# The keys' sums of four token tiles in one run, six weight sums moved from the keys into the perceptron, later numerators

## The chip, the cores and the metric

The kernel runs on one core of one Trainium2 chip. The metric is the time of one execution on the device in microseconds; lower is better. The engines are named as in the profile: PE (TensorE; PEld is its weight load), DVE (VectorE), ACT (ScalarE), POOL (GpSimd) and SP (SyncE, which here issues nearly all transfers; the ACT queue issues the stores of the queries' exponentials). Each of the first four works through its own queue in order, and so does SP.

## What is computed

A transformer block in fp32 on 2048 tokens of 1024 features: linear attention with a learned softmax feature map (32 heads of 32), then a perceptron of width 3584.

```python
def _A_ref(x, wqkv, w_phi, wo):
    q, k, v = qkv[0], qkv[1], qkv[2]
    pq = jnp.einsum("bhsd,hdf->bhsf", q, w_phi)
    pk = jnp.einsum("bhsd,hdf->bhsf", k, w_phi)
    phi_q = jnp.concatenate([_softmax(pq, axis=-1), _softmax(-pq, axis=-1)], axis=-1)
    phi_k = jnp.concatenate([_softmax(pk, axis=-1), _softmax(-pk, axis=-1)], axis=-1)
    kv = jnp.einsum("bhsf,bhsd->bhfd", phi_k, v)
    z  = jnp.einsum("bhsf->bhf", phi_k)
    num = jnp.einsum("bhqf,bhfd->bhqd", phi_q, kv)
    den = jnp.einsum("bhqf,bhf->bhq", phi_q, z)[..., None] + 1e-6
    o = num / den
    return (o as B, S, D) @ wo

h = x + _A_ref(_layernorm(x, axis=-1), A_wqkv, A_w_phi, A_wo)
h2 = h + relu(_layernorm(h) @ w1) @ w2
```

## The kernel before

**Products.** Every large product is made three times, from a high part and a remainder of each operand (mm3, L181 to L184: high by high, high by remainder, remainder by high), as matmuls of 128 x 128 by 128 x 512. Weights come raw from memory; ACT copies the high part (L125), and DVE or POOL makes the remainder (L129). Ten split weights (RW) and six raw ones (RR) are held. A matmul triple, one mm3, is a *step*; in the attention an item has eight steps, in the perceptron four. The work beside the products is put by hand at a step: `when(step, f, ...)` and `do(item, k, f, ...)` issue `f` there, and each engine then runs it in the order of issue, as soon as its inputs are there.

**Order of the stages.** Token tiles 0 to 7 (first half): keys and values in four slabs of 256 columns (items kv, 4 x 8), then queries in two slabs (items q, 2 x 8). Tiles 8 to 15 the same (second half, steps 384 to 767). Then the output product (wo, from step 768), which runs beside the attention's numerators, and from step 1024 (up0) the perceptron: first half `up_item`, 784 steps, second half `down_item`. The perceptron's products are of Strassen's kind with seven products (m in 1 to 7) of 2 x 2 blocks, so that some weight blocks are sums of blocks.

**Keys.** Per tile and slab: kv_first (L423; values to `vt`, maxima, minima and differences), kv_exp (11 steps after the item's start), kv_second (13; the map `kphi`), kv_z (18; POOL adds to the sums `zacc`) and kv_third (L456): eight small matmuls, run as 16 passes of 128x32 by 128x64, that add this tile's part of kv in two PSUM banks (`ac`). They need `vt` and `kphi` of that tile, and they stand at step 8(n + d) + 22 for item n, where d is 2, 1, 0, 2, 1, 0, 1, 0 over the eight tiles of a slab and half. So three, three and two tiles fall on one step. After the last slab z_sum (L484) and kv_turn (L478, L481) bring the sums into place.

**Weight sums.** t_load, t_sum and t_store (L348 to L366) make the sums of weight blocks that the perceptron's products use: per unit a load of 512 KB by SP, four subtractions on POOL (L363, 128 x 256 each, in place, in four consecutive steps), and a store of 512 KB by SP. There are 56 units, 28 of w1 and then 28 of w2; `sums_at` gives the step of each. The buffer is one of two pairs at a time (`b` in the pool tsum, `xn` of the layer norm, or `b` in the fold pool), by `home`.

**Attention.** at_load (L555; SP) brings a query unit u of 32 (512 KB); for some units the denominators are made early, in the keys' second half (EARLY: early_load, early_sums L582 on POOL, early_reduce L586 on DVE, at_cross, at_den, early_scale L590). at_scale (L629 and L634, POOL) divides, at_turn (L640, DVE) transposes, and at_num (L643, L653), for each odd u, makes the numerators of two units in two `ac` banks, which ACT (L660) and at_low (L670, DVE) bring into `oT`. For u < 8 the start of a unit is 8(last_kv + 4) + 19u // 2, and at_num stands 30 + `slack` steps after it. q_first (L514) needs one of two buffers `qe`, from which the ACT queue stores the exponentials (`ed`, L532); two tiles later the buffer is needed again.

**Perceptron, first half.** far_pair (L786) uses one buffer `y2` of the pool mp, for the second half of the tokens' layer norm; its last far_store stands at step up0 + 324.

Of the kernel before, what the change touches and what calls it, by code (L numbers as in the profile page):

```python
# [9 lines left out]
F32 = mybir.dt.float32  # L10
# [5 lines left out]
P = 128  # L16
S = 2048
D = 1024
# [4 lines left out]
HT = NT // 2  # L23
# [117 lines left out]
def kernel(  # L141
# [47 lines left out]
    def do(n, k, f, *args):  # L189
        at[n, k].append((f, args))  # L190
# [69 lines left out]
    fp_ln = kps.enter_context(tc.tile_pool(name="xn", bufs=2, side="right"))  # L260
    kp = kps.enter_context(tc.tile_pool(name="kp", bufs=2, side="right"))
    tsp = kps.enter_context(tc.tile_pool(name="tsum", bufs=1, side="right"))
    folds = ExitStack()
    fp = folds.enter_context(tc.tile_pool(name="fold", bufs=2))
# [82 lines left out]

    def t_load(w, p, j, home):  # L348
        cols = slice(256 * j, 256 * (j + 1))
        b = fp_ln.tile([P, D], F32, name="xn").rearrange("p (a f) -> p a f", a=4) if home == 2 else \  # L350
            (tsp, fp)[home].tile([P, 4, 256], F32, name="b", bufs=2)
        src = (w1 if w == 1 else w2)[2 * p:2 * p + 2, :, :, cols]
        sp.dma_start(b, src.rearrange("a b p f -> p (a b) f"))
        for r in range(2):
            for c in range(2):
                tsum[w, p, j, r, c] = b[:, 2 * c + r if w == 1 else 2 * r + c, :]
        tsum[w, p, j] = b
# [65 lines left out]
    def kv_first(key, ps):  # L423

        pk = ps[:, 0:256].rearrange("p (h f) -> p h f", f=32)
        vt = kp.tile([P, 256], F32, name="vt", bufs=5)
        act.activation(vt, ps[:, 256:512], AF.Copy)
        v_of[key] = vt
        m = kp.tile([P, 2, 8], F32, name="kmx", bufs=2)
        v.tensor_reduce(out=m[:, 0, :], in_=pk, op=ALU.max, axis=AX.X)  # L430
        v.tensor_reduce(out=m[:, 1, :], in_=pk, op=ALU.min, axis=AX.X)
        e = kp.tile([P, 8, 2, 32], F32, name="ke", bufs=2)
        v.tensor_sub(e[:, :, 0, :], pk, m[:, 0, :, None].to_broadcast([P, 8, 32]))
        v.tensor_sub(e[:, :, 1, :], m[:, 1, :, None].to_broadcast([P, 8, 32]), pk)
        e_of[key] = e
# [4 lines left out]
    def kv_second(key):  # L440
        e = e_of.pop(key).rearrange("p h s f -> p (h s) f")
        sm = kp.tile([P, 16], F32, name="ksm", bufs=2)
        v.tensor_reduce(out=sm, in_=e, op=ALU.add, axis=AX.X)
        v.reciprocal(sm, sm)
        phi = kp.tile([P, 16, 32], F32, name="kphi", bufs=4)
        v.tensor_mul(phi, e, sm[:, :, None].to_broadcast([P, 16, 32]))
        phi_of[key] = phi.rearrange("p h f -> p (h f)")

# [57 lines left out]
    def kv_item(key, keys):  # L506
        ps = yield from project(key[2], keys)
        kv_first(key, ps)
# [441 lines left out]
    def item(gen, *args, keys):  # L950
        items.append((gen, args + (keys,)))
        steps.extend((k,) for k in keys)
        return len(items) - 1
# [11 lines left out]
    for b, tiles in enumerate(groups):  # L965
        for hf in range(2):

            pairs = b == 0 and hf == 0
            for j in range(0, 4, 2 if pairs else 1):
# [3 lines left out]
                for half in range(2):  # L973
                    n = item(wo_pair, tiles[j:j + 2], hf, half, keys=[("wo", hf, 4 * half + k // 2) for k in range(8)])
# [26 lines left out]
    def when(step, f, *args):  # L1001

        if step < 8 * first_up:
            do(step // 8, step % 8, f, *args)
        else:
            do(first_up + (step - 8 * first_up) // 4, step % 4, f, *args)
# [4 lines left out]
    for t in range(1, NT):  # L1011
        n = t - 1 if t < HT else q_n[1, t - HT] + 1
# [34 lines left out]
    for (hf, s, t), n in kv_n.items():  # L1047
        when(8 * n + 11, kv_exp, (hf, s, t))
        when(8 * n + 13, kv_second, (hf, s, t))
        when(8 * n + 18, kv_z, (hf, s, t))  # L1050
        when(8 * (n + (2, 1, 0, 2, 1, 0, 1, 0)[t % HT]) + 22, kv_third, (hf, s, t))
        if hf == 1 and t == NT - 1:
            do(n + 3, 7, z_sum, s)
            do(n + 3, 7, kv_turn, s)
# [67 lines left out]
    for (sl, t), n in q_n.items():  # L1122
# [3 lines left out]
        b, i = place_of[t]  # L1126
# [2 lines left out]
            when(8 * n + (48, 48, 48, 72)[b], sm_load, b)  # L1129
    for u in range(32):  # L1130
        start = 8 * (a0 + u) - 4 if u >= 8 else 8 * (last_kv + 4) + 19 * u // 2
        slack = 6 if u < 6 else 4 if u >= 8 else 0
        late_ = 0 if u < 8 or u in EARLY else 3

        for step, f, *args in ((-8, at_load), (6, at_sums, 0), (10, at_reduce, 0), (9, at_sums, 1), (12, at_reduce, 1),
                               (14 + late_, at_cross), (16 + late_, at_den), (18 + late_, at_inverse), (20 + late_, at_scale),
                               (26 if u < 8 else 27, at_turn)):
            if u not in EARLY or f in (at_load, at_scale, at_turn):
                when(max(start + step, 8 * (last_kv + 4)), f, u, *args)
        if u % 2:  # L1140
            when(start + 30 + slack, at_num, u)
            when(start + 32 + slack, at_low, u)
        if u in EARLY:
            slab, after = EARLY[u]
            start = 8 * (kv_n[1, slab, NT - 1] + 4) + after
            for step, f in ((0, early_load), (9, early_sums), (14, early_reduce), (17, at_cross), (20, at_den), (22, early_scale)):
                when(start + step, f, u)
# [22 lines left out]
    up0 = 8 * first_up  # L1170
# [12 lines left out]
    def up_step(b, p, m):  # L1183

        return up0 + 4 * (up_n[b, p, m] + 1 - first_up)

    for j, m in enumerate(UP):

        for g in range(2):
            step = up0 + (8 * j + (-62, -29)[g] if j < 4 else 6 * (j - 4) + 4 + 2 * g)  # L1190
# [4 lines left out]
            step = up_step(0, NP - 1, m) + 2 * j  # L1195
# [4 lines left out]
    for b in range(2):  # L1200
# [7 lines left out]

    sixth, fifth = (10, 19, 28, 37, 46, 55), (10, 21, 32, 43, 54)
    sums_at = [30, 39, 47, 55] + [64 * i + k for i in (1, 2, 3) for k in sixth] + \  # L1210
        [266, 276, 286, 296, 332, 342, 352, 362, 372] + [64 * i + k for i in (6, 7, 8, 9) for k in (sixth, fifth)[i % 2]] + [638, 646, 655]
    for n, (w, p, j) in enumerate((w, p, j) for w in (1, 2) for p in range(NP) for j in range(2)):
        step = sums_at[n]
        half_on = sums_at.index(64 * 6 + 10)
        home = (0, 0, 1, 1)[n % 4] if step < 236 else (0, 0, 2, 2)[(n - half_on) % 4] if n >= half_on else 0
        when(step - (7 if 256 < step < 400 else 15), t_load, w, p, j, home)
        for k in range(4):
            when(step + k, t_sum, (w, p, j), k)
        when(step + 6, t_store, w, p, j)

    for b in range(2):
        for m in DOWN:
            n = down_n[b, m, NP - 1] + 1
            name, more = {1: "x1", 5: "x4", 6: "x2", 4: "x3"}.get(m), \
# [109 lines left out]
```

## Time and profile before

| | us |
|---|---|
| median of 3 runs | 1869.45 (1868.44 to 1871.39) |
| the profiled execution | 1867.49 |
| its span, first to last instruction | 1865.7 |
| PE busy | 1855.9 (99%) |
| DVE busy | 1065.1 (57%) |
| POOL busy | 978.9 (52%) |
| ACT busy | 770.9 (41%) |

Times inside the trace count from the first instruction. The stages in the trace: keys of the first half up to about 220 us, queries to about 330, keys of the second half to about 520, queries to about 608, output product to about 795, perceptron to 1329 and 1866. PE's busy time holds overlapping matmuls, so that 99% doesn't say that each runs at its best; the distance from one start to the next says more. The granted clock is 1.00 throughout. A row of the timeline gives start, duration, engine, line, operation, output and inputs, shape and count, and in brackets the idle time before and what ended it. A row of waits gives who waited for whom, the total in us, how often, and the longest.

### The profile page before, as it was taken

To read this page: it belongs to the slowest core of one execution; us is meant where nothing else is said; L and a number is where in the kernel's file an instruction comes from. 1 tells how busy PE (TensorE), PEld (TensorE's weight loads), DVE (VectorE), ACT (ScalarE), POOL (GpSimd) and SP (SyncE) were. 2 spreads that over 40 slices of the span, in tenths; PEclk is the share of its full clock that TensorE was granted. 3 is DMA by queue.
4 is the path that set the end of the run, shared out by engine and by line. 5 is a ranking of instruction groups with operands and counts; after the bars stand their busy time and mean duration, and the time that the engine had idled before them with its cause. 6 is when DMAs were issued, how large, how long until landed. Compare 5 with 4: busy or idle time off the path is not lost.

```text
span 1865.7 us, 28872 instructions
## 1 busy us (share of the span) xinstructions
PE 1855.9 (99%) x10088; PEld 1515.6 (81%) x10088; DVE 1065.1 (57%) x1651; ACT 770.9 (41%) x1379; POOL 978.9 (52%) x987
## 2 busy tenths in 40 slices
PE   9999999999999999999999999999999999999999
PEld 7777788887777777888888888888888888888887
DVE  7787678678679877575555653453434333343333
ACT  5322244233333343355455554444444444444442
POOL 4887745889956988343333222222344444444443
PEclk9999999999999999999999999999999999999999
DMA  7888799666676776888888976666677777777775
GB/s 229 288 292 285 237 288 266 194 196 201 209 229 194 247 244 206 283 271 231 248 257 265 328 240 184 194 206 198 229 222 215 216 218 238 237 218 215 216 217 177
DMA packets 334722, 435.13 MB, mean 233 GB/s; under 512 B 28784, under 2 KB 194672, under 8 KB 334576
## 3 DMA queue, kind: packets, MB, share of 16 engines
q1 hardware_dynamic: 300784, 416.51, 71.8%
q10 hardware_dynamic: 33792, 16.78, 3.1%
q8 instruction: 79, 1.29, 0.3%
q14 instruction: 67, 0.55, 0.1%
HBM read 295.31 MB, written 137.89 MB: 232 GB/s over the span
## 4 chain that ended last, share of the span: by engine, by line
PE 94%; DVE 3%; POOL 1%; issue 1%; ACT 0%; DMA 0%; SPq 0%; POOLq 0%; DVEq 0%
PE mm L182 24%; PE mm L183 24%; PE mm L184 24%; PE ac L182 4%; PE ac L184 4%; PE ac L183 4%; PE tp L182 2%; PE tp L183 2%; PE tp L184 2%; PE tp L246 1%; PE ac L465 1%; PE ac L653 1%; POOL w L129 1%; DVE qsm L537 1%; DVE qe L524 0%
## 5 line engine op out<-in xcount | busy, mean ns | idle before, releaser
L129 POOL TENSOR_TENSOR w<-raw,w 128x512 fp32r<-128x512 f32 x353 | 470.4, 1335 | 689.0 <-ACT w L125 664.3
L125 ACT ACTIVATE w<-raw 128x512 fp32r<-128x512 f32 x686 | 408.5, 626 | 506.9 <-PE mm L184 232.0
L129 DVE TENSOR_TENSOR w<-raw,w 128x512 fp32r<-128x512 f32 x333 | 269.1, 808 | 510.5 <-ACT w L125 504.6
L182 PE MATMUL mm<-w,xT 128*128 128x512 f32 x768 | 305.4, 398 | 0.0
L183 PE MATMUL mm<-w,xT 128*128 128x512 f32 x768 | 299.9, 391 | 1.0 <-POOL w L129 0.6
L184 PE MATMUL mm<-w,xT 128*128 128x512 f32 x768 | 299.3, 390 | 0.0
L183 PE MATMUL mm<-hT,w 128*128 128x512 f32 x672 | 261.4, 389 | 0.0
L182 PE MATMUL mm<-hT,w 128*128 128x512 f32 x672 | 261.4, 389 | 0.0
L184 PE MATMUL mm<-hT,w 128*128 128x512 f32 x672 | 261.4, 389 | 0.0
L182 PEld LDWEIGHTS mm<-w,xT 128*128 128x128 f32 x768 | 144.2, 188 | 34.9 <-issue 3.7
L184 PEld LDWEIGHTS mm<-w,xT 128*128 128x128 f32 x768 | 144.2, 188 | 30.7
L183 PEld LDWEIGHTS mm<-w,xT 128*128 128x128 f32 x768 | 144.3, 188 | 30.2 <-POOL w L129 1.2
L363 POOL TENSOR_TENSOR b<-b 128x256 f32<-128x256 f32 x176 | 143.5, 816 | 48.1 <-DMA b<-in_w_dram 39.9
L182 PE MATMUL mm<-w 128*128 128x512 f32 x392 | 152.5, 389 | 0.0
L183 PE MATMUL mm<-w 128*128 128x512 f32 x392 | 152.5, 389 | 0.0
L184 PE MATMUL mm<-w 128*128 128x512 f32 x392 | 152.5, 389 | 0.0
L183 PEld LDWEIGHTS mm<-hT,w 128*128 128x128 f32 x672 | 126.2, 188 | 26.2
L184 PEld LDWEIGHTS mm<-hT,w 128*128 128x128 f32 x672 | 126.2, 188 | 26.2
L182 PEld LDWEIGHTS mm<-hT,w 128*128 128x128 f32 x672 | 126.2, 188 | 26.1
L184 PEld LDWEIGHTS mm<-w 128*128 128x128 f32 x392 | 73.6, 188 | 15.3
L182 PEld LDWEIGHTS mm<-w 128*128 128x128 f32 x392 | 73.6, 188 | 15.3
L183 PEld LDWEIGHTS mm<-w 128*128 128x128 f32 x392 | 73.6, 188 | 15.2
(173 smaller groups left out, 3107.5 us busy)
## 6 DMA issues: line engine op xcount, KB each, us to landing
raw<-t SPq DMA_DIRECT2D x224, 256.0 KB, 3.9
raw<-ad SPq DMA_DIRECT2D x196, 256.0 KB, 3.0
raw<-in_w_dram SPq DMA_DIRECT2D x168, 256.0 KB, 3.1
ad<-c SPq DMA_DIRECT2D x112, 256.0 KB, 3.6
b<-in_w_dram SPq DMA_DIRECT2D x44, 512.0 KB, 5.7
t<-b SPq DMA_DIRECT2D x44, 512.0 KB, 5.0
ad<-s SPq DMA_DIRECT2D x84, 256.0 KB, 3.8
ed<-qe ACTq DMA_DIRECT2D x64, 256.0 KB, 4.6
```

The source lines that it names most:

```text
L125: nc.scalar.activation(w[:, 0, :], raw[1], AF.Copy)
L129: eng.tensor_tensor(out=w[:, 1, :], in0=raw[1], in1=w[:, 0, :].bitcast(F32), op=ALU.subtract)
L182: pe.matmul(ps, a_hi, b_hi, start=first, stop=False, skip_group_check=more)
L183: pe.matmul(ps, a_hi, b_lo, start=False, stop=False, skip_group_check=more)
L184: pe.matmul(ps, a_lo, b_hi, start=False, stop=last, skip_group_check=more)
L246: pe.transpose(pt[:, k, :], xn[:, (4 * j + k) * P:(4 * j + k + 1) * P], ident)
L363: pool.tensor_tensor(out=tsum[*u, *out], in0=tsum[*u, *a], in1=tsum[*u, *b], op=ALU.subtract)
L465: pe.matmul(kv_ps[s][g][32 * i:32 * (i + 1), 0:64], vt[:, 32 * h:32 * (h + 1)], phi[:, 64 * h:64 * (h + 1)], start=first, stop=last)
L537: v.tensor_reduce(out=sm[:, 0].rearrange("p s (a c) -> p a s c", a=4), in_=e_of.pop((s, t)), op=ALU.add, axis=AX.X)
L653: pe.matmul(banks[g][32 * c:32 * (c + 1), 256 * j:256 * (j + 1)], kvL[rows, 2 * q + h // 4, 32 * (h % 4):32 * (h % 4 + 1)], phT_of[u - 1 + ...
```

## The change

Four edits.

1. kv_third stands at 8(n + 3 - t % 4) + 22: tiles 0 to 3 of a slab and half fall on one step, and tiles 4 to 7. `vt` has six buffers instead of five, `kphi` five instead of four.
2. In the second half's keys the weight sums stand five to a slab in the second and third slab (six in the third before), three in the last (five before), and the three at the steps 638, 646 and 655 are no longer there.
3. Six units, the last of w2, stand in the perceptron's first half, at up0 + 480 + 36i, with the buffer y2.
4. The slack of u = 6 and 7 is 6 instead of 0. at_num is there for odd u alone, so at_num(7) and at_low(7) stand six steps later.

```diff
     def t_load(w, p, j, home):
         cols = slice(256 * j, 256 * (j + 1))
-        b = fp_ln.tile([P, D], F32, name="xn").rearrange("p (a f) -> p a f", a=4) if home == 2 else \
-            (tsp, fp)[home].tile([P, 4, 256], F32, name="b", bufs=2)
+        if home > 1:
+            b = fp_ln.tile([P, D], F32, name="xn") if home == 2 else mp.tile([P, D], F32, name="y2", bufs=1)
+            b = b.rearrange("p (a f) -> p a f", a=4)
+        else:
+            b = (tsp, fp)[home].tile([P, 4, 256], F32, name="b", bufs=2)
...
-        vt = kp.tile([P, 256], F32, name="vt", bufs=5)
+        vt = kp.tile([P, 256], F32, name="vt", bufs=6)
...
-        phi = kp.tile([P, 16, 32], F32, name="kphi", bufs=4)
+        phi = kp.tile([P, 16, 32], F32, name="kphi", bufs=5)
...
-        when(8 * (n + (2, 1, 0, 2, 1, 0, 1, 0)[t % HT]) + 22, kv_third, (hf, s, t))
+        when(8 * (n + (3 - t % 4)) + 22, kv_third, (hf, s, t))
...
         start = 8 * (a0 + u) - 4 if u >= 8 else 8 * (last_kv + 4) + 19 * u // 2
-        slack = 6 if u < 6 else 4 if u >= 8 else 0
+        slack = 6 if u < 8 else 4
...
     sixth, fifth = (10, 19, 28, 37, 46, 55), (10, 21, 32, 43, 54)
     sums_at = [30, 39, 47, 55] + [64 * i + k for i in (1, 2, 3) for k in sixth] + \
-        [266, 276, 286, 296, 332, 342, 352, 362, 372] + [64 * i + k for i in (6, 7, 8, 9) for k in (sixth, fifth)[i % 2]] + [638, 646, 655]
+        [266, 276, 286, 296, 332, 342, 352, 362, 372] + [64 * i + k for i, places in ((6, sixth), (7, fifth), (8, fifth), (9, (14, 28, 44))) for k in places] + \
+        [up0 + 480 + 36 * i for i in range(6)]
     for n, (w, p, j) in enumerate((w, p, j) for w in (1, 2) for p in range(NP) for j in range(2)):
         step = sums_at[n]
         half_on = sums_at.index(64 * 6 + 10)
-        home = (0, 0, 1, 1)[n % 4] if step < 236 else (0, 0, 2, 2)[(n - half_on) % 4] if n >= half_on else 0
+        home = 3 if step > up0 else (0, 0, 1, 1)[n % 4] if step < 236 else (0, 0, 2, 2)[(n - half_on) % 4] if n >= half_on else 0
         when(step - (7 if 256 < step < 400 else 15), t_load, w, p, j, home)
```

## The prediction

> **What bounds the kernel now.** I read the page first, then TensorE's own waits, then the busy time by stage, then the timelines where those waits fall.
>
> ```profile
> span 1865.7 us, 28872 instructions
> PE 1855.9 (99%) x10088; PEld 1515.6 (81%) x10088; DVE 1065.1 (57%) x1651; ACT 770.9 (41%) x1379; POOL 978.9 (52%) x987
> ...
> PE ac L653 <- DVE qe L640: 1.6, 1, 1.6
> ...
> PE ac L465 <- ACT w L125: 0.7, 1, 0.7
> PE mm L183 <- POOL w L129: 0.6, 1, 0.6
> ...
> PE tp L481 <- DVE kd L475: 0.3, 1, 0.3
> ```
>
> TensorE is busy for 99% of the span. Beside the first 17 us it waits at four places, all quoted. Only two things can shorten this kernel: those four waits, and work that fills TensorE's stream without being one of the large matmuls. The stream has a fixed beat, which a stage without small matmuls shows:
>
> ```profile
> 330.00:520.00 190.00, 189.02 (x1316) 150.99 (x1315) 133.32 (x258) 63.90 (x144) 169.75 (x169) 1.00 0.63 197
> ...
> 795.00:1329.00 534.00, 534.00 (x2386) 442.06 (x2385) 270.67 (x335) 264.63 (x447) 151.91 (x113) 1.00 0.77 234
> ```
>
> The columns after the length are busy time (and count) of PE, PEld, DVE, ACT and POOL. In the perceptron's first half (the lower row) 2386 matmuls less 32 tiny ones take 534.0 us: 0.227 us each, at clock 1.00; a step of three is 0.68 us. POOL is at 28% there, and at 89% in the second half of the keys (the upper row).
>
> **The keys' sums (kv_third).** Nothing is removed: 1024 passes stay 1024. Only the number of times changes that TensorE leaves the large matmuls for them.
>
> ```profile
> L465 PE MATMUL ac<-kphi,vt 128*32 128x64 f32 x1024 | 19.5, 221 | 0.7 <-ACT w L125 0.7
> ...
> 79.66 0.39 PE L184 MATMUL mm<-w,xT 128*128 128x512 f32 x1
> 79.98 0.65 PE L465 MATMUL ac<-kphi,vt 128*32 128x64 f32 x32
> 80.56 0.50 PE L182 MATMUL mm<-w,xT 128*128 128x512 f32 x1
> 80.90 0.40 PE L183 MATMUL mm<-w,xT 128*128 128x512 f32 x1
> ...
> 96.78 0.39 PE L184 MATMUL mm<-w,xT 128*128 128x512 f32 x1
> 97.10 0.88 PE L465 MATMUL ac<-kphi,vt 128*32 128x64 f32 x48
> ...
> 98.25 0.40 PE L183 MATMUL mm<-w,xT 128*128 128x512 f32 x1
> ...
> 99.20 0.39 PE L184 MATMUL mm<-w,xT 128*128 128x512 f32 x1
> ```
>
> A token tile is 16 passes (1024 over 64 tiles). Two tiles in a run: from the last large matmul before to the second after, 80.90 - 79.66 = 1.24 us, less two beats (0.45) = 0.79 us. Three tiles: 98.25 - 96.78 = 1.47, less 0.45 = 1.02 us. So a tile costs 0.23 us, and a run of any length 0.33 us more. The next four matmuls come at 0.2375 instead of 0.227 (98.25 to 99.20), another 0.04. Before, eight tiles of a slab and half go in runs of 3, 3 and 2; after, in 4 and 4, so each of the eight slab halves loses one run: 8 x 0.33 = 2.6 us at least, 8 x 0.37 = 3.0 at most. I take **2.9**, near the upper end, because the tail is seen behind the run.
>
> The first tile of a group now waits eight steps longer for its sum, which is why the buffers of vt and kphi grow by one each (1 KB and 2 KB of a partition). The last tile of each group keeps its distance: its kphi is made at step 13 after its item's start, its sum goes at 22. The fifth kphi buffer is written again at step 53 of a half, and the run that frees it stands at 46: seven steps or 4.8 us, as before (45 against 38). I cost that at nothing; if DVE were to wait there, only its kphi would come later, and TensorE reads that nine steps on.
>
> **The sums off the slab edge.** In the second half of the keys 25 weight sums (t_sum, four instructions each) become 19: one fewer in the third slab, two fewer in the last, and the three at its end are gone. Each is 4 x 0.74 us on POOL:
>
> ```profile
> 330.00:520.00 190.00, 73.66 (x89) 1.00 0.63 197
> ...
> 505.18 0.74 POOL L363 TENSOR_TENSOR xn<-xn 128x256 f32<-128x256 f32 x1
> 506.41 2.40 POOL L582 TENSOR_TENSOR xl<-xl,zb 128x1024 f32<-128x1024 f32 x1
> ...
> 508.85 1.22 DVE L586 TENSOR_REDUCE xtz<-xl 128x32 f32<-128x1024 f32 x1 [2.01 <-POOL xl L582]
> 510.99 0.71 DVE L446 TENSOR_TENSOR kphi<-ke,ksm 128x512 f32<-128x512 f32 x1
> ...
> 510.73 0.43 PE L465 MATMUL ac<-kphi,vt 128*32 128x64 f32 x16
> ...
> 512.20 0.50 PE L182 MATMUL mm<-w,xT 128*128 128x512 f32 x1
> ...
> 518.93 0.35 DVE L590 RECIPROCAL smx<-qden 128x32 f32<-128x32 f32 x1 [4.84 <-POOL qden L621]
> ```
>
> The first row is those sums alone: 73.7 us of POOL's 169.75. Six fewer take about 17.7 us from it. At the end of the last slab POOL runs late, the early queries' product (L582) stands behind sums, DVE's reduction waits for that, and the last tile's kphi stands behind the reduction, until 511.70. TensorE, at 511, waits. That run of 32 takes 1.47 us from its start to the next large matmul (510.73 to 512.20), against 0.58 at the undisturbed one above (79.98 to 80.56), so the wait costs **0.9**; TensorE's own row counts 0.7 of it, the lower end. With the sums of steps 630 and 638 gone from POOL's queue ahead of L582, kphi should come 3 to 4 us sooner, and in a run of four the last tile is read another 0.5 us later. The wait of L481 for kd has the same origin: ahead of kd in DVE's queue stands a reciprocal that waits 4.84 us, to 518.93, for a quotient that POOL delivers behind the same sums. It goes too: **0.3**.
>
> **The second query slab.** SyncE and ScalarE queues are passed here as well:
>
> ```profile
> 523.30 0.51 SPq L366 DMA_DIRECT2D t<-b  x1
> 523.86 5.80 SPq L555 DMA_DIRECT2D qe<-ed  x5
> ...
> 538.11 0.69 DVE L523 TENSOR_TENSOR qe<-mm,qmx 128x512 f32<-128x512 f32 x1 [5.43 <-DMA ed<-qe]
> ...
> 545.33 3.24 ACT L125 ACTIVATE w<-raw 128x512 fp32r<-128x512 f32 x6 [1.00 <-PE mm L184]
> ...
> 550.49 0.39 PE L182 MATMUL mm<-w,xT 128*128 128x512 f32 x1
> 551.83 0.40 PE L184 MATMUL mm<-w,xT 128*128 128x512 f32 x1
> ```
>
> SyncE stores the last sum at 523.30, once POOL has made it, and only then issues five loads of the attention (at_load). They share the DMA engines with the stores of the queries' exponentials (ed); one of those lands late, and DVE idles 5.43 us for its buffer. ScalarE stands in order behind those exponentials, so the six weight copies of the second query slab begin at 545.33, and POOL's remainders after them come late: two beats take 1.34 us instead of 0.45, **0.9** lost. Without the three sums SyncE is free of that store; the loads go as soon as the keys' buffers under them are free, between the last kv_third (512.2) and the turn that follows at 519.8: 4 to 12 us earlier, while DVE still has slack to catch up. I take the whole 0.9; the other end is nothing.
>
> **The later numerators.** Only u = 7 is odd with slack 0, so at_num(7) and at_low(7) go from steps 760 and 762 to 766 and 768.
>
> ```profile
> 580.54 1.09 PE L653 MATMUL ac<-qe,kvL 64*32 64x256 f32 x32
> 581.56 0.50 PE L182 MATMUL mm<-w,xT 128*128 128x512 f32 x1
> ...
> 590.62 0.66 PE L653 MATMUL ac<-qe,kvL 64*32 64x256 f32 x16
> 593.44 0.50 PE L182 MATMUL mm<-w,xT 128*128 128x512 f32 x1
> ...
> 591.60 1.19 DVE L640 STREAM_TRANSPOSE qe<-qe 128x1024 f32<-128x1024 f32 x1
> ```
>
> The run that waits takes 2.82 us, an undisturbed one 1.02: **1.8** lost, since DVE ends the transpose at 592.79. Six steps are 4.1 us, more than the lateness of 2.2, so the wait goes even if nothing else improves. What is late next: at_low(7) now stands behind the last query's maxima on DVE (four of 0.68) and its product is read at step 780, 12 steps or 8.2 us after 768. It needs some 3.6 us. Covered, unless DVE is more than 4.5 us late.
>
> **The six sums in the perceptron's first half.** They add six loads and six stores of 512 KB to SyncE's queue, and 17.7 us to POOL, in bursts of 3 us every 36 steps (24.5 us). What hides them (a stretch of that stage, 1122 to 1250 us):
>
> ```profile
> ACT w L125 <- PE mm L184: 25.3, 17, 1.6
> ...
> L129 POOL TENSOR_TENSOR w<-raw,w 128x512 fp32r<-128x512 f32 x23 | 30.2, 1314 | 94.9 <-ACT w L125 90.9 <-DMA ad<-s 4.0
> ```
>
> ScalarE's copies wait for TensorE to free one of ten weight places, so a weight is split about nine units (4 steps each, 24 us) ahead of its use. A burst of 3 us, and a store that holds SyncE for it, stay inside that. I cost it at nothing; without the cover, 17.7 us. The tile y2, which the loads use, is stored for the last time at step 324 of the stage; the first load stands at 465. What POOL still has to spare there is in the last row: 94.9 of 128 us.
>
> **Sum.** 2.9 + 0.9 + 0.3 + 0.9 + 1.8 = 6.8 us. The profiled execution took 1867.5, which gives 1860.7; it was 2.0 below the median of the runs shown (1869.45), and the median gives **1862.6**.
>
> **The rivals.** *The collision moves instead of going.* The attention's loads, earlier, meet the ed store of an earlier query tile; DVE idles as before and the weights of the second query slab stay late: 1862.6 + 0.9 = 1863.5; if at_num(7) still waits as well, 1865.3. For it: the loads' 2.5 MB do not shrink. The Trainium skill, DMA: Bandwidth & Descriptors, Issuing engines are not separate DMA queues, says that transfers started by different engines interleave on the same 16 DMA engines; the 5.43 us above agree. Against it: DVE also idles 4.8 us ahead of that stretch in the trace of before, which it can now use.
>
> *VectorE is the bound from 541 to 611.*
>
> ```profile
> 541.00:611.00 70.00, 67.83 (x431) 52.33 (x430) 68.45 (x102) 29.03 (x53) 49.52 (x59) 1.00 0.70 206
> ```
>
> DVE is busy for 68.45 of these 70 us, so what TensorE gains ahead of it could come back as a wait further on, and only the changeovers stay: 1869.45 - 2.9 = 1866.6. Against: the 5.4 us of idling lie just before.
>
> *The changeovers are priced by the pass, not by the run.* Then only the waits go: 1869.45 - 3.9 = 1865.5. The two rows above speak against it.
>
> *Slower: POOL's sums block VectorE in the perceptron.* In the keys it looks so:
>
> ```profile
> 498.83 1.48 DVE L446 TENSOR_TENSOR kphi<-ke,ksm 128x512 f32<-128x512 f32 x1
> ```
>
> The same instruction took 0.71 us at 510.99, with POOL idle. If each of the 24 new instructions held up one of DVE's and TensorE felt all of it, 24 x 0.74 = 17.7 us, less the 6.8: 1880.3. It decides from 10.5 us on, 0.44 for each. Against: DVE idles half of that stage and TensorE never waits in it. The Trainium skill, SBUF — State Buffer, Who interferes with whom, makes this a rule: an instruction of VectorE with two SBUF inputs and one of GpSimd that reads SBUF shut each other out until the first ends. The two kphi rows agree; no row here shows TensorE waiting for it.
>
> **How the numbers follow.** Forecast 0.68, the collision moves 0.15, VectorE bound 0.07, no cheaper changeovers 0.06, slower 0.04. About 0.2% (3.7 us) is what a measurement of this kernel can tell from no change. The forecast and most of the first rival are faster by more; the third is at the line; the second is within: 0.84, 0.12, 0.04. The low end takes every term at its upper end (7.0) and 1.4 of spread between runs; the high end reaches the VectorE rival: 1861.0 to 1866.5.
>
> **What would show it.** Runs of kv_third of 64 passes, 16 of them, each some 1.25 us; no wait of TensorE left at L465, L481, L183 and L653 between 500 and 600 us; the at_load row before 520 us, no idling of several us on DVE for ed; six groups of L363 on y2 after 1100 us with TensorE gapless. Wrong, if a new wait stands in the perceptron, or if DVE's idling for ed only moves.

## The result, and the profile after

| | before | after |
|---|---|---|
| median of ten runs, us | 1869.52 (1868.32 to 1872.12) | 1864.66 (1864.36 to 1865.06) |
| ratio | | 0.9971 (95%: 0.9963 to 0.9980) |
| span of the profiled execution, us | 1865.7 | 1862.7 |

The change gains 4.9 us by the medians; 6.8 were forecast. The two profiled executions differ by 3.0 us only, because the one of before took 1867.49 us, less than any of its ten timed runs. What follows compares traces, so its terms add up to about 3.

The page of the changed kernel, and TensorE's waits in it:

```profile
span 1862.7 us, 28867 instructions
PE 1852.3 (99%) x10088; PEld 1515.2 (81%) x10088; DVE 1069.7 (57%) x1651; ACT 771.3 (41%) x1379; POOL 982.0 (53%) x987
...
PE tp L246 <- ACT xn L239: 2.4, 1, 2.4
PE tp L1257 <- POOL ones L1253: 1.6, 1, 1.6
PE mm L183 <- POOL w L129: 1.0, 3, 0.7
PE mm L183 <- DVE w L129: 0.8, 1, 0.8
PE ac L656 <- DVE qe L643: 0.4, 1, 0.4
PE mm L183 <- POOL w L404: 0.4, 1, 0.4
```

From L351 on, the lines stand three or four lower than before (kv_third is now L468, at_num L656). The waits at kv_third and at kd are gone, and that at the numerators fell from 1.6 to 0.4. But L183, a matmul that reads a weight's remainder, now waits four times for POOL or DVE instead of once (the row with L404 is the start of the kernel). So part of the gain became other waits. Where, the start of the same large matmul in each trace shows (us; the last column is the fastest kernel of the experiments):

| step | before | after | difference | e8 |
|---|---|---|---|---|
| 0 | 13.40 | 13.71 | +0.31 | 13.51 |
| 384, keys of the second half | 311.42 | 312.07 | +0.65 | 310.10 |
| 640, queries | 500.31 | 499.37 | -0.94 | 496.80 |
| 704, second query slab | 547.08 | 545.12 | -1.96 | 542.55 |
| 712 | 554.69 | 551.80 | -2.89 | 549.24 |
| 768, output product | 598.33 | 593.61 | -4.72 | 591.04 |
| 1024, perceptron | 794.72 | 791.69 | -3.04 | 787.28 |
| last | 1861.62 | 1858.57 | -3.05 | 1854.16 |

The difference at the first row is the landing of the first tokens, which is not the change's: DVE begins on their second half at 5.38 us before and at 5.68 after. Over the traces of this document the first large matmul stands anywhere from 13.3 to 14.2 us, and at 15.6 in e7, where the granted clock is also 0.50 from 9.73 to 13.13 us.

The keys: one of the new runs, and a slab's edge (timeline, TensorE, then POOL):

```profile
104.20 0.39 PE L184 MATMUL mm<-w,xT 128*128 128x512 f32 x1
104.52 1.10 PE L468 MATMUL ac<-kphi,vt 128*32 128x64 f32 x64
...
105.89 0.40 PE L183 MATMUL mm<-w,xT 128*128 128x512 f32 x1
...
169.79 0.39 PE L182 MATMUL mm<-w,xT 128*128 128x512 f32 x1
170.84 0.50 PE L183 MATMUL mm<-w,xT 128*128 128x512 f32 x1 [0.67 <-POOL w L129]
...
167.92 1.18 POOL L366 TENSOR_TENSOR b<-b 128x256 f32<-128x256 f32 x1
169.07 2.97 POOL L129 TENSOR_TENSOR w<-raw,w 128x512 fp32r<-128x512 f32 x2
```

A run of 64 passes takes 105.89 - 104.20 - 0.45 = 1.24 us (1.25 forecast). At 170 TensorE is at step 196, the fifth weight of a new slab, and waits: POOL was still at a weight sum until 169.10 and made two remainders after it. Such a wait, with a slower first beat behind it, stands at the steps 132, 196 and 452 (0.46, 0.95 and 0.46 us in all), and two smaller ones, 0.14 and 0.10 us, at 263 and 582; before there was none of them.

The queries (timeline of SP, DVE and ACT):

```profile
513.54 9.84 SPq L558 DMA_DIRECT2D qe<-ed  x5
...
522.02 0.69 DVE L526 TENSOR_TENSOR qe<-mm,qmx 128x512 f32<-128x512 f32 x1 [2.32 <-DMA ed<-qe]
...
540.55 4.09 ACT L125 ACTIVATE w<-raw 128x512 fp32r<-128x512 f32 x6 [2.54 <-PE mm L184]
```

The attention's loads start 10.3 us sooner (513.54 against 523.86). DVE's idling for ed is 2.3 instead of 5.4 us and comes 16 us earlier, while there is slack; the second query slab's weight copies now wait for TensorE, as they should, and TensorE has no wait at step 709. (The row of before, at 545.33, names TensorE as well, for 1.00 us. There ScalarE's queue issued two stores of ed from 544.36 to 545.29, and the six copies then ran without a gap: it was late, not waiting.)

The start of the output product (timeline of PE and DVE):

```profile
603.14 0.39 PE L182 MATMUL mm<-w,oT 128*128 128x512 f32 x1
604.36 0.50 PE L183 MATMUL mm<-w,oT 128*128 128x512 f32 x1 [0.83 <-DVE w L129]
604.70 0.40 PE L184 MATMUL mm<-w,oT 128*128 128x512 f32 x1
605.02 0.66 PE L656 MATMUL ac<-qe,kvL 64*32 64x256 f32 x16
606.10 0.67 PE L656 MATMUL ac<-qe,kvL 64*32 64x256 f32 x16 [0.41 <-DVE qe L643]
606.70 0.50 PE L182 MATMUL mm<-w,oT 128*128 128x512 f32 x1
...
602.17 1.20 DVE L540 TENSOR_REDUCE qsm<-qe 128x32 f32<-128x1024 f32 x1
603.40 0.35 DVE L541 RECIPROCAL qsm<-qsm 128x32 f32<-128x32 f32 x1
603.67 0.63 DVE L129 TENSOR_TENSOR w<-raw,w 128x512 fp32r<-128x512 f32 x1
```

at_num(7) no longer waits: 2.9 us less up to step 761, of which 1.1 is its run itself, which stands later. But 15 steps on TensorE waits for a weight whose remainder DVE makes at 603.67, behind the queries' reductions: from 603.14 to 604.70, less two beats, 1.1 us. at_num(9), right behind, takes 1.68 us (605.02 to 606.70) instead of 1.02. So 1.76 of the 1.8 us come back.

Busy time in the three stages shown of before (us, busy of PE, PEld, DVE, ACT, POOL), and the six moved units on POOL:

```profile
330.00:520.00 190.00, 189.81 (x1328) 153.15 (x1327) 136.87 (x267) 66.60 (x149) 155.88 (x152) 1.00 0.57 176
541.00:611.00 70.00, 68.76 (x435) 53.21 (x434) 67.50 (x95) 30.52 (x56) 49.66 (x59) 1.00 0.69 211
795.00:1329.00 534.00, 534.00 (x2386) 442.22 (x2385) 271.26 (x334) 264.95 (x448) 170.11 (x135) 1.00 0.80 245
...
L366 POOL TENSOR_TENSOR y<-y x24: 727/742/1185, 1118.5 to 1246.4; 128x256 f32<-128x256 f32 x24
```

In the perceptron POOL has 18.2 us more to do (170.11 against 151.91) and TensorE 2386 matmuls in 534.00 us, as before. From step 1024 to the last large matmul it takes 1066.9 us in both.

### The profile page after: what moved, and what is told of

Same layout as the page of the kernel before. It is cut to its first block, busy times and chain, and to the rows that moved or that the text cites. A ratio compares the mean times of both kernels' runs of the same rounds, so it can differ in the third digit from the quotient of the medians.

```text
span 1862.7 us, 28867 instructions
## 1 busy us (share of the span) xinstructions
PE 1852.3 (99%) x10088; PEld 1515.2 (81%) x10088; DVE 1069.7 (57%) x1651; ACT 771.3 (41%) x1379; POOL 982.0 (53%) x987
## 4 chain that ended last, share of the span: by engine, by line
PE 93%; DVE 4%; POOL 1%; issue 1%; ACT 0%; DMA 0%; SPq 0%; POOLq 0%; DVEq 0%; ACTq 0%
PE mm L182 24%; PE mm L183 24%; PE mm L184 24%; PE ac L182 4%; PE ac L184 4%; PE ac L183 4%; PE tp L184 2%; PE tp L183 2%; PE tp L182 2%; PE tp L246 1%; PE ac L468 1%; POOL w L129 1%; PE ac L656 1%; DVE qsm L540 1%; DVE qe L643 0%
## 5 line engine op out<-in xcount | busy, mean ns | idle before, releaser
L129 DVE TENSOR_TENSOR w<-raw,w 128x512 fp32r<-128x512 f32 x333 | 274.0, 823 | 511.0 <-ACT w L125 502.0
L183 PE MATMUL mm<-w,xT 128*128 128x512 f32 x768 | 300.2, 391 | 1.4 <-POOL w L129 1.0
L183 PE MATMUL mm<-hT,w 128*128 128x512 f32 x672 | 261.7, 389 | 0.0
L183 PEld LDWEIGHTS mm<-w,xT 128*128 128x128 f32 x768 | 144.4, 188 | 31.8 <-POOL w L129 2.8
L366 POOL TENSOR_TENSOR b<-b 128x256 f32<-128x256 f32 x164 | 134.3, 819 | 49.4 <-DMA b<-in_w_dram 32.3
L183 PE MATMUL mm<-w 128*128 128x512 f32 x392 | 152.6, 389 | 0.0
L183 PEld LDWEIGHTS mm<-hT,w 128*128 128x128 f32 x672 | 126.2, 188 | 26.2
L183 PEld LDWEIGHTS mm<-w 128*128 128x128 f32 x392 | 73.6, 188 | 15.2
```

The source lines that it names most:

```text
L129: eng.tensor_tensor(out=w[:, 1, :], in0=raw[1], in1=w[:, 0, :].bitcast(F32), op=ALU.subtract)
L183: pe.matmul(ps, a_hi, b_lo, start=False, stop=False, skip_group_check=more)
L366: pool.tensor_tensor(out=tsum[*u, *out], in0=tsum[*u, *a], in1=tsum[*u, *b], op=ALU.subtract)
```

## The experiments

The comparison is with the kernel before, run beside each; the interval is that of the ratio. Where a run is set against the changed kernel or against e8, the two ran at different times (e9 and e10 also on another chip than e1 to e8), and their intervals overlap or touch. There the traces decide, and "by the traces" means from the first large matmul to the last.

**e1: the runs of four alone**

```diff
-        vt = kp.tile([P, 256], F32, name="vt", bufs=5)
+        vt = kp.tile([P, 256], F32, name="vt", bufs=6)
-        phi = kp.tile([P, 16, 32], F32, name="kphi", bufs=4)
+        phi = kp.tile([P, 16, 32], F32, name="kphi", bufs=5)
-        when(8 * (n + (2, 1, 0, 2, 1, 0, 1, 0)[t % HT]) + 22, kv_third, (hf, s, t))
+        when(8 * (n + (3 - t % 4)) + 22, kv_third, (hf, s, t))
```

> The kernel before with the keys' sums in runs of four tiles (and the larger vt and kphi) alone. Theory: sixteen runs of 64 passes instead of 24 of 48 and 32 save 0.40 us in each of eight slab halves, 3.2 us; but the run that stood two steps ahead of a slab's edge (step 62) had given POOL and DVE time for the next slab's weights, so that without it TensorE waits at the fifth weight of a new slab, some 2 us in all as in the changed kernel (steps 132, 196, 256, 452): about 1.1 us faster than before. Rival: those waits come from the moved weight sums, not from the runs: 3.2 us faster, and no wait at steps 132 and 196.

1866.32 us against 1869.02, ratio 0.9989 (0.9981 to 0.9998). Among its waits:

```profile
PE mm L183 <- POOL w L129: 1.6, 5, 0.7
```

The ratio's interval holds both expectations (0.4 to 3.6 us); the median gains 2.7 us, nearer to the rival's 3.2, and by the traces it is 0.9. The trace decides on the cause: the waits at the steps 132, 196 and 452 are here, of the same size (jumps of 0.34, 0.83 and 0.35 us against before), without a moved weight sum. They come with the runs. Another 1.3 us is lost at the steps 645 to 647, at the edge to the queries' first slab, where the changed kernel, with fewer sums there, loses nothing.

One thing more, which neither expectation has: the wait at 551 us (step 709) is gone here too (0.89 us), although SyncE issues the attention's loads at 524.81, no earlier than before. DVE's idling for ed is 4.1 us in two pieces instead of 5.4 in one.

**e2: the moved weight sums alone**, shown against the changed kernel

```diff
-        vt = kp.tile([P, 256], F32, name="vt", bufs=6)
+        vt = kp.tile([P, 256], F32, name="vt", bufs=5)
-        phi = kp.tile([P, 16, 32], F32, name="kphi", bufs=5)
+        phi = kp.tile([P, 16, 32], F32, name="kphi", bufs=4)
-        when(8 * (n + (3 - t % 4)) + 22, kv_third, (hf, s, t))
+        when(8 * (n + (2, 1, 0, 2, 1, 0, 1, 0)[t % HT]) + 22, kv_third, (hf, s, t))
-        slack = 6 if u < 8 else 4
+        slack = 6 if u < 6 else 4 if u >= 8 else 0
```

> The kernel before with the moved weight sums alone (six in the perceptron's first half, fewer near the ends of slabs). Theory: the waits at 511, 519 and 551 us go (0.9, 0.3 and 0.9), the one at at_num(7) stays at 1.5 to 2 us because DVE is as late there, and no wait comes at a slab's edge in the keys: 1.8 to 2.2 us faster. Rival: the waits at the slabs' edges are the sums' doing: they appear here too, and the gain is near nothing. In the perceptron's first half TensorE has no wait by both.

1864.95 us, ratio 0.9978 (0.9969 to 0.9987): 4.1 us. In the trace the three waits go (jumps of -0.89, -0.46 and -0.90 us at the steps 655, 664 and 709), there is none at a slab's edge, a small one is new (0.4 us at step 939, in the output product), and the one at at_num(7) falls by 0.91 instead of staying:

```profile
PE ac L656 <- DVE qe L643: 0.7, 1, 0.7
```

That last gain was not expected in this size: DVE, ahead of the queries, makes up part of its lateness. The medians show more than the 2.8 us of the traces, as with the whole change.

**e3: the later numerators alone**

```diff
-        slack = 6 if u < 6 else 4 if u >= 8 else 0
+        slack = 6 if u < 8 else 4
```

> The kernel before with the later numerators of u = 7 alone. The prediction's step: 1.8 us faster, since nothing is late next. Theory: VectorE is 6 us late at the start of the output product, so the wait goes from at_num(7) to the weights of the output product and to at_num(9), 12 to 20 steps later, at about the same price: within 0.5 us of before.

1869.26 us against 1869.02, ratio 0.9998 (0.9989 to 1.0007): nothing. The prediction's step falls. The timeline shows the two waits that took the place of the one:

```profile
607.38 0.50 PE L183 MATMUL mm<-w,oT 128*128 128x512 f32 x1 [1.20 <-DVE w L129]
...
609.12 1.11 PE L653 MATMUL ac<-qe,kvL 64*32 64x256 f32 x16 [0.41 <-DVE qe L640]
```

**e4: the changed kernel without the later numerators**

```diff
-        slack = 6 if u < 8 else 4
+        slack = 6 if u < 6 else 4 if u >= 8 else 0
```

> The changed kernel with the later numerators alone undone. Theory: at_num(7) waits some 2 us for DVE's transpose, and the two waits that the changed kernel has at 603 and 606 us (1.1 and 0.65 us) go: within 0.5 us of the changed kernel. The prediction's step: 1.8 us slower than the changed kernel.

1863.76 us, ratio 0.9973 (0.9962 to 0.9983): 0.9 us below the changed kernel's median, 0.4 by the traces. The waits at the steps 782 and 783 are gone, and at_num(7) waits:

```profile
PE ac L656 <- DVE qe L643: 1.2, 1, 1.2
```

So the later numerators did not pay in the kernel that they are part of; if anything they cost.

**e5: two fold runs moved to the slabs' edges**

```diff
-FOLD_STEPS = 31, 64, 104, 144, 176, 206, 232
+FOLD_STEPS = 31, 64, 126, 144, 190, 206, 232
```

> The changed kernel with two fold runs (64 small matmuls each, which are there anyway) moved from steps 104 and 176 to 126 and 190, two steps ahead of a slab's edge. Theory: a run of small matmuls there gives the next slab's weights their time, as the keys' sums had done: the waits at steps 132 and 196 (0.45 and 0.95 us with the slow start after each) go, 1.2 to 1.4 us faster than the changed kernel, those at 256 and 452 stay. Rival: DVE's four transposes behind each fold (0.67 us each) delay DVE's share of the weights by as much: no gain, and the wait moves from a weight of POOL's to one of DVE's.

1863.85 us, ratio 0.9968 (0.9955 to 0.9980), 0.8 below the changed kernel, 0.5 by the traces. The wait at step 132 goes (-0.34), the one at 196 stays (TensorE, then POOL):

```profile
169.06 0.39 PE L182 MATMUL mm<-w,xT 128*128 128x512 f32 x1
170.26 0.50 PE L183 MATMUL mm<-w,xT 128*128 128x512 f32 x1 [0.81 <-POOL w L129]
...
150.34 0.74 POOL L366 TENSOR_TENSOR b<-b 128x256 f32<-128x256 f32 x1 [5.54 <-DMA b<-in_w_dram]
```

One edge for the theory, one against it. It waits for POOL, not for DVE, so the rival's reason is not it either. The edit moved more than the pause: with the folds SyncE's transfers moved too, and POOL idled 5.54 us for a weight sum's load, to 150.34 (1.79 us, to 146.12, in the changed kernel). From there on POOL has no gap, and its remainders for the new slab begin at 168.94, against 169.07, although TensorE came to the pause (step 190) at 163.26 us, 2.45 sooner. That the late load cancelled the pause is argued from these rows; no run here separates the two. That the run before the edge was what hid the late weights is therefore shown by e1 against before, and at one edge here.

**e6: no weight sum in a slab's last ten steps**

```diff
-    sums_at = [30, 39, 47, 55] + [64 * i + k for i in (1, 2, 3) for k in sixth] + \
+    sums_at = [30, 39, 47, 55] + [64 * i + k for i in (1, 2, 3) for k in sixth[:5]] + \
...
-        [64 * i + k for i, places in ((6, sixth), (7, fifth), (8, fifth), (9, (14, 28, 44))) for k in places] + \
+        [64 * i + k for i, places in ((6, sixth[:5]), (7, fifth), (8, fifth), (9, (14, 28, 44))) for k in places] + \
-        [up0 + 480 + 36 * i for i in range(6)]
+        [up0 + 430 + 32 * i for i in range(10)]
```

(The two buffer pairs of the first half also change places, so that their turns still fit.)

> The changed kernel with no weight sum in the last ten steps of a slab in the first half's keys and in the first slab of the second half (steps 119, 183, 247 and 439 are left out, and ten units instead of six stand in the perceptron's first half, 32 steps apart). Theory: POOL has 3 us more for the weights at these edges, and the waits at steps 132, 196, 256 and 452 (2.1 us in all) go or fall under a quarter: 1.5 to 2.1 us faster than the changed kernel; no wait in the perceptron. Rival: the weights are late because their places come free only with the last tile's matmuls, whatever POOL does: the waits stay, and the time too.

1862.48 us, ratio 0.9959 (0.9945 to 0.9973), 2.2 below the changed kernel, 1.7 by the traces. No wait for a weight is left in the keys; of all of L183's waits after the start one remains, that of the output product:

```profile
PE mm L183 <- DVE w L129: 1.0, 1, 1.0
```

So the weights at the edges were late for POOL's sums, and the places that come free with the last tile would have been early enough.

**e7: the output product's first remainders on POOL**

```diff
-            odd = key[0] == "a" or key[0] in ("kv", "w1", "wo") and self.done % 2 or \
+            odd = key[0] == "a" or key[0] in ("kv", "w1", "wo") and self.done % 2 and key[:2] != ("wo", 0) or \
```

> The changed kernel with the remainders of the output product's first weights (eight units, of which four were DVE's) all on POOL. Theory: VectorE is 6 us behind at the start of the output product and holds one of these weights; on POOL it is in time, so the wait at 603 us (1.1) goes and that of at_num(9) (0.65) falls: 1.1 to 1.7 us faster than the changed kernel. Rival: POOL is as late there, or DVE's lateness shows at at_num(9) instead: within 0.4 us of the changed kernel.

1863.36 us, ratio 0.9965 (0.9952 to 0.9978), 1.3 below the changed kernel, 1.75 by the traces. In the trace both waits go (-0.99 and -0.66 at the steps 782 and 783). DVE's place in the order, not the weights' arrival, had held TensorE.

**e8: both**, that is the two diffs of e6 and e7 on the changed kernel

> The changed kernel with both of the last two edits (no sums at the slabs' edges, the output product's first remainders on POOL). Theory: the gains add, 2.6 to 3.8 us faster than the changed kernel, and TensorE waits nowhere for more than 0.3 us after the first 60 us. Rival: either edit fails as in its own run.

1860.73 us, ratio 0.9950 (0.9937 to 0.9963): 3.9 below the changed kernel, 4.2 by the traces: somewhat more than the two edits alone (2.2 and 1.3, or 1.7 and 1.75) and than the upper end of the expectation. This is the fastest kernel here, and these are all of TensorE's waits in it:

```profile
PE tp L1257 <- POOL ones L1253: 1.6, 1, 1.6
PE tp L246 <- ACT xn L239: 1.2, 1, 1.2
PE mm L183 <- POOL w L404: 0.4, 1, 0.4
```

**e9: e8 without the later numerators**

```diff
-        slack = 6 if u < 8 else 4
+        slack = 6 if u < 6 else 4 if u >= 8 else 0
```

> The fastest kernel so far (no sums at the slabs' edges, the output product's first remainders on POOL) with the later numerators alone undone. Theory: they cost the changed kernel 0.9 us only because DVE held a weight of the output product; that weight is POOL's now, so here they pay: at_num(7) waits 1 to 2 us for DVE, nothing later takes it back, and the kernel is 1 to 2 us slower than with them. Rival: DVE catches up in that wait and the time is the same within 0.4 us, so that the later numerators pay nothing in any setting.

1862.20 us, ratio 0.9966 (0.9952 to 0.9979): 1.5 slower than e8, 1.6 by the traces, so here the later numerators pay. But not by the wait that was expected. at_num(7) does not wait in e9; a weight of the output product does (0.9 us, step 782). The timelines of e8 and then e9 show why:

```profile
585.96 1.30 POOL L129 TENSOR_TENSOR w<-raw,w 128x512 fp32r<-128x512 f32 x1 [2.27 <-ACT w L125]
585.99 1.31 ACT L125 ACTIVATE w<-raw 128x512 fp32r<-128x512 f32 x2
...
586.80 1.09 ACT L663 ACTIVATE oT<-ac 128x512 fp32r<-128x512 f32 x2 [2.28 <-PE ac L656]
587.77 1.68 ACT L125 ACTIVATE w<-raw 128x512 fp32r<-128x512 f32 x3
588.48 1.30 POOL L129 TENSOR_TENSOR w<-raw,w 128x512 fp32r<-128x512 f32 x1 [4.29 <-ACT w L125]
```

With the numerators at step 760, ScalarE's two evictions (L663) stand ahead of the output product's weight copies, wait for TensorE, and POOL begins its row of remainders 2.5 us later.

**e10: e8 with the runs of three, three and two**

```diff
-        when(8 * (n + (3 - t % 4)) + 22, kv_third, (hf, s, t))
+        when(8 * (n + (2, 1, 0, 2, 1, 0, 1, 0)[t % HT]) + 22, kv_third, (hf, s, t))
```

> The fastest kernel so far with the keys' sums back in runs of three, three and two tiles. Theory: no wait at the slabs' edges is left for the runs to hide or to uncover, so this is the price of eight changeovers alone: 3.2 us slower (8 x 0.40), in steps of 0.40 per slab half. Rival: the runs of four have waits of their own for vt or kphi: less than 2.5 us slower.

1863.78 us, ratio 0.9972 (0.9962 to 0.9982): 3.05 slower than e8. The spans differ by 3.6, of which 0.4 stand ahead of the first large matmul; so eight runs fewer are worth 3.1 to 3.2 us, 0.38 to 0.40 each, and no run of four waits for vt or kphi.

## Why the prediction was right or wrong

**The price of the runs was nearly right, and what they covered was left out.** Forecast 2.9 us, range 2.6 to 3.0; measured 3.1 to 3.2 (e10). The failed step is "Only the number of times changes that TensorE leaves the large matmuls for them": it books all of the time as gain. The one place where the prediction looks for a price, "I cost that at nothing", looks at vt and kphi alone, and there it was right. What the old run at step 62 did beside its own work was to hold TensorE back for 1.0 us just where the next slab's weights were being split. Between steps 128 and 640 the waits at the edges take back some 2.4 us: e8, with none of them, is 2.4 us ahead of the changed kernel at step 640, start counted off. The trace of before could have told: POOL at 89% of the stage, and a matmul run two steps ahead of each edge, are both in it.

**The waits at 511, 519 and 551 us went as forecast.** 0.9, 0.3 and 0.9 against 0.89, 0.46 and 0.90 (e2). The collision moved earlier, as the first rival had it, but at 2.3 us it found DVE with slack. For the wait at 551 the reason given, the earlier loads, is not shown to be the only one: in e1 it went without them, and why stays open.

**The later numerators were worth nothing, not 1.8 us.** The failed step is "Covered, unless DVE is more than 4.5 us late". It followed only at_low(7), which was in time. It left out what else DVE holds at that place: a remainder of the output product's weights, and the transpose for at_num(9). This is the second rival, "VectorE is the bound from 541 to 611" (0.07), in part: DVE is busy for 67.5 of those 70 us still, and what TensorE gained ahead of it came back. e7 shows it by taking the weight off DVE.

**The perceptron's six sums cost nothing, as forecast**; ten cost nothing either (e6, e8; 1066.9 us from step 1024 on in each). The rival on the slow side, 17.7 us, is out, though POOL's sums do lengthen there now and then (742 ns in the median, 1185 at most): the eight that take 1062 ns or more all begin while DVE is in an elementwise instruction of two inputs, the sixteen of 727 to 743 ns do not. That agrees with the rule of the Trainium skill named beside it (SBUF — State Buffer, Who interferes with whom); in this stage none of it reached TensorE. One of the prediction's two kphi rows was misread: at 510.99 POOL was not idle, its sum ran to 511.14. The pair still points the right way, since the seven kphi products of before with no POOL instruction beside them take 0.69 us each, and the longest beside one 2.77.

**The sum.** Of 6.8, the trace keeps 3.0: 2.4 for the three waits (from step 640 to 712 the difference grows by 1.95 us, though a run that is 0.45 us longer now stands there), some 0.8 of the runs' 3.2, some 0.1 of the numerators' 1.8, and 0.3 less for a later start. By the medians it is 4.9, since before's ten runs lie 0.8 to 4.6 us above the one profiled, and scatter more than the changed kernel's (1864.36 to 1865.06). The granted clock is part of that (last section); the rest is not explained here. So it is in part luck that the measured time lies well inside the forecast's range: two of the five terms came to little, and the 3.0 us that the trace keeps would have put the median at the range's upper end, 1869.5 - 3.0 = 1866.5.

## What to carry to other kernels

On a stream without gaps, work that one takes out or moves has a second value: the time that it gave to whatever is only just ready behind it. Before it is costed as pure gain, look which transfer, split or eviction is due within its length, and how full the engine that makes it is. And when a wait on a busy engine is taken away, follow that whole engine for the next 15 steps, not the one product that was moved: here the same lateness of DVE showed at the next weight.

## What the runs showed of the hardware

After the two waits of e3 TensorE ran at half its clock for 3.4 us, though together the waits lasted 1.6 us only:

```profile
610.75 0.63 PE L183 MATMUL mm<-w,oT 128*128 128x512 f32 x1
611.17 0.63 PE L184 MATMUL mm<-w,oT 128*128 128x512 f32 x1
611.60 0.63 PE L182 MATMUL mm<-w,oT 128*128 128x512 f32 x1
...
609.10:612.50 3.40, 3.38 (x22) 2.09 (x23) 3.37 (x5) 3.18 (x9) 3.40 (x4) 0.50 1.06 327
```

The matmuls start 0.43 us apart instead of 0.227, and the granted clock of the stretch is 0.50 (the last row). That cost some 1.5 us on top of the waits: 1.1 over the five matmuls behind the second run of at_num(9), and 0.4 in that run itself (1.11 us at 609.12, against 0.67 in the changed kernel). In the changed kernel, with waits of 0.83 and 0.41 us at the same place, the matmuls behind them keep their beat.

Not every execution has such a stretch. Of the 29 executions of the kernel before beside e1 to e4, the 14 of 1869.55 us and more show a mean granted clock of 0.999 or 0.998, the 15 of 1869.02 us and less show 1.000, as do all ten of the changed kernel. One stretch like that of e3 is 1.7 us, or 0.0009 of the span. The median of those 15 is 1868.33 us, 0.7 below that of all 29, so about that much of the 4.9 us is an estimate of what the clock adds. The trace of before has no such stretch, so where in the kernel the clock falls in the other executions stays open.
